# Attention backward of a branchformer layer: dP products in groups of four key chunks, with the remainder channels at four row positions of TensorE

## The chip, the cores and the metric

The kernel runs on one core of a Trainium2 chip. The metric is the device time of one launch in microseconds (us), the median of several runs. A profiled execution, taken by the hardware profiler, shows every instruction with its engine, line, start and duration. The engines are called PE (TensorE, matrix products; PEld are its weight loads), DVE (VectorE), ACT (ScalarE), POOL (GpSimd) and SP (SyncE, which here issues DMAs).

## The reference

The layer has two branches, attention and a gated convolution, which are merged by a depthwise convolution and a product. The kernel returns the output and the gradients of all eight inputs. Sizes: B = 2 sequences, T = 4000 tokens, D = 144 channels, K = 5 taps, all in bfloat16. What matters here is the attention and its gradient:

```python
xa = _layernorm(x, axis=-1)
qkv = jnp.einsum('btd,de->bte', xa, w_qkv)
q, k, v = (qkv[..., :D].copy(), qkv[..., D:2 * D].copy(), qkv[..., 2 * D:].copy())
scores = jnp.einsum('btd,bsd->bts', q, k) * D ** (-0.5)
p = _softmax(scores, axis=-1)
attn = jnp.einsum('bts,bsd->btd', p, v)
glob = jnp.einsum('btd,de->bte', attn, w_att_out)
...
return x + jnp.einsum('btc,cd->btd', m, w_merge)

def reference(x, w_qkv, ..., grad_out):
    _out, _vjp = jax.vjp(_f, x, w_qkv, w_att_out, w_mlp_in, dw_csgu, w_mlp_out, dw_merge, w_merge)
    _grads = _vjp(grad_out)
    return (_out, *_grads)
```

The backward pass needs, for every query block, the probabilities P (after the scores), dP = (gradient of attn) times v transposed, and dS = (dP - delta) * P, where delta is a number for each query.

## The kernel before, in words

Each sequence is cut into NB = 32 blocks of PB = 125 tokens (tokens are dealt out so that a block has one token of each partition's run). A query block is called a tile. The keys of a sequence are taken in eight chunks of CH = 500 columns, and two chunks make a pair. The key and value weights are folded into the query side, so that scores and dP are both products of a small transposed query tile with the normalized input `xa`, transposed. D = 144 does not fit the 128 rows of PE: the first 128 channels lie in `xaT_m` (128 x 4000), and the other DR = 16 in rows 0 to 15 of `R` (128 x 4000; its rows 16 to 111 hold the remainder channels of the output gradient for other products). Every product over the channels is therefore two matmuls: one with `xaT_m` and one with `R`, whose query side has zeros in the rows that don't count.

The two sequences are worked one after the other: a prologue (layernorm, transposes), then the attention loop `phase_att`, then a merge. Inside the loop, a few steps of one tile are:

- `jit_mm(i)` (L648) forms the query side `qb` (125 x 2 x 256; index 0 for scores, index 1 for dP; columns 144 to 255 are zero) in PSUM, and ACT copies it to one of three buffers. `jit_tr(i)` (L660) transposes it on PE into `qt` with four slots of 125 columns: slots 0 and 1 are main channels and remainder of the scores, slots 2 and 3 those of dP.
- `S_pair(i, c2)` (L673): four matmuls for a pair of chunks (L683 main, L684 remainder), a DVE operation of 1000 columns with a running minimum (L688, L690), and an exponential on ACT (L691) into `Pbuf`.
- `rescale(i)` (L693) brings earlier pairs to the final maximum (L700, L702) and starts a transposing DMA of P on SP's queue (L703).
- `Y_half(i, h)` (L705): 32 matmuls in two halves over the transposed P, then the reciprocal of the row sums, delta, and copies.
- `dP_pair(i, c2)` (L727): four matmuls for a pair of chunks, main and remainder alternating (L733, L734), then two DVE operations of 500 columns that form dS in `Sbuf` (L739).
- `Z_half` (L749), the same as Y over the transposed dS, and `zt_tr`.
- `X_group` (L780): products that gather the gradient of `xa` for three key blocks over the last two tiles (L794), added to `acc` by DVE (L800).
- `local(upto)` (L809) draws on a list of units of the convolution branch, so many as the share of the loop that has passed.

In iteration t the loop writes out the scores of tile t, Y and dP of tile t-1, Z of tile t-2 and X of tiles t-3 and t-2, in eight steps (L826 to L856): score pairs in steps 0 to 3, dP pairs in steps 4 to 7, and the other work between them. A planner turns this order into each engine's instruction order: it may draw an instruction ahead where an earlier one would have to wait, by its own estimates.

The PSUM pool `ps_sg` (L627) has two buffers of two banks each. A score pair and a dP pair each take one; a buffer comes free when the exponential (scores) or the dS operations (dP) have read it. The pool `ps_w` (three buffers) serves the other products, and `ps_yz` Y and Z.

In the prologue, `xat(g)` (L340) transposes `xa` and writes `xaT_m` and `R` for 1000 columns. SP's queue carries in the loop the transposing DMAs of P and dS and the stores of Y, Z and `ug`; in the prologue of the second sequence also the loads of `xo` and the stores of the first sequence's output.

Of the kernel before, what the change touches and what calls it, by code (L numbers as in the profile page):

```python
# [7 lines left out]
BF = mybir.dt.bfloat16  # L8
F32 = mybir.dt.float32
ACT = mybir.ActivationFunctionType  # L10
ALU = mybir.AluOpType
# [4 lines left out]
DR = 16  # L16
PB = 125
CH = 500
# [275 lines left out]
def pre_pieces(k, W, b, S, pst):  # L294
# [4 lines left out]
    if True:  # L299
# [49 lines left out]

        def go_rem():  # L350
            nc.gpsimd.tensor_copy(S.go_r[:], go_q[:, :, 128:D])
# [264 lines left out]
def phase_att(k, W, b, S, A, M):  # L616
# [6 lines left out]
    with ExitStack() as es:  # L623
# [20 lines left out]
        xaTm, R, xaa = S.xaT_m, S.R, S.xa_aug  # L644
# [3 lines left out]
        def jit_mm(i):  # L648
# [8 lines left out]
            nc.scalar.copy(qb[:, :, 0:D], pj[:].rearrange("p (a b) -> p a b", b=D))  # L657
            QB[i] = qb
# [68 lines left out]
        def dP_pair(i, c2):  # L727
            qt = QT[i]
            ps = ps_sg.tile([PB, 2, 512], F32, tag="sg")
            for h in range(2):  # L730
                c = 2 * c2 + h
                cs = slice(c * CH, (c + 1) * CH)
                nc.tensor.matmul(ps[:, h, 0:CH], qt[:, 2, :], xaTm[:, cs], start=True, stop=False)  # L733
                nc.tensor.matmul(ps[:, h, 0:CH], qt[:, 3, :], R[:, cs], start=False, stop=True)  # L734
            for h in range(2):
                c = 2 * c2 + h
                psrc = Pbuf[0:PB, i % NPB, c * 512:(c + 1) * 512].rearrange("p (a b) -> p a b", b=128)[:, :, 0:PB]
                sdst = Sbuf[0:PB, i % NDB, c * 512:(c + 1) * 512].rearrange("p (a b) -> p a b", b=128)[:, :, 0:PB]
                nc.vector.scalar_tensor_tensor(sdst, ps[:, h, 0:CH].rearrange("p (a b) -> p a b", b=PB), DL[i][:], psrc, op0=ALU.subtract, op1=ALU.mult)  # L739
# [63 lines left out]
        def ok(i):  # L803
            return 0 <= i < NB
# [11 lines left out]
        for t in range(NB + 1):  # L816
# [5 lines left out]
            def x(n):  # L822
                for _ in range(n):
                    if xg:
                        X_group(*xg.pop(0))
            for s in range(8):  # L826
                if s < 4 and ok(t):
                    S_pair(t, s)
                if s >= 4 and ok(t - 1):
                    dP_pair(t - 1, s - 4)  # L830
                if t == NB and s == 4:
                    M.late_y()
                if s == 0:
                    if ok(t - 3):
                        zt_tr(t - 3)
                    x(1)
                elif s == 1:
                    if ok(t + 1):
                        jit_mm(t + 1)
                    x(1)  # L840
                elif s in (2, 3):
                    if ok(t - 1):
                        Y_half(t - 1, s - 2)
                    if s == 3 and ok(t):
                        rescale(t)
                elif s == 4:
                    if ok(t + 1):
                        jit_tr(t + 1)
                    x(1)
                elif s == 5:  # L850
                    x(1)
                else:
                    if ok(t - 2) and t < NB:
                        Z_half(t - 2, s - 6)
                    x(1)
                local(-(-n_units * (8 * t + s + 1) // (8 * (NB - 1))))  # L856
# [415 lines left out]
def kernel(ctx, tc, x, w_qkv, w_att_out, w_mlp_in, dw_csgu, w_mlp_out, dw_merge, w_merge, grad_out,  # L1272
# [20 lines left out]
    R = bx.tile([128, T], BF, name="R")  # L1293
    go_r = bx.tile([PB, NB + 6, DR], BF, name="go_r")
# [7 lines left out]
    for b, S in enumerate(SS):  # L1302
        S.xaT_m, S.R, S.go_r, S.goT, S.acc, S.rstd_x = xaT_m, R, go_r, goT, acc, rstd[b]
        for nm in ("Yn", "ug", "Zn"):
            setattr(S, nm + "_d", tc.dram_tile([PB, NB, D], BF, name="%s_d%d" % (nm, b)))
# [155 lines left out]
```

## Time and profile before

| | |
|---|---|
| median of 3 runs | 1478.05 us (1475.49 to 1479.26) |
| profiled execution, device time | 1477.11 us |
| its span, first to last instruction | 1475.3 us |
| mean granted clock of PE | 0.985 |
| matmuls | 16184 |
| busy, share of the span | PE 93%, PEld 80%, DVE 82%, ACT 58%, POOL 19% |
| attention loop of the first sequence | about 59 to 660 us |
| attention loop of the second sequence | about 768 to 1370 us |

Busy times come from one execution. A matmul's recorded duration holds its latency in the array; what it costs PE is the distance from its start to the start of the next one. Lines such as L734 are those of the kernel file before the change. In a group of instructions, "x512" is the count, followed by the busy time in us and the mean duration of one in ns, and after the next bar the idle time of the engine just ahead of them with what ended it.

### The profile page before, as it was taken

The page shows a single profiled execution, that of the slowest core. Times are in us where ns is not written, and L with a number is a line of the kernel's source. Part 1 is how long each engine was busy: PE and PEld are TensorE (multiplying, and loading weights), DVE is VectorE, ACT ScalarE, POOL GpSimd, SP SyncE. Part 2 cuts the span into 40 slices and gives each one's busy share as a digit, 9 for nine tenths or more (in the row PEclk, how much of TensorE's full clock was granted, in tenths as well). Part 3 has the DMA queues.
Part 4 walks back from the last instruction along what each step waited for, and adds up shares of the span by engine and source line. Part 5 has one row for each costly group of instructions (what it writes and reads, how often), then busy time and mean ns, then how long its engine had stood idle before and what let it go on. Part 6 is the DMA issues. An engine that isn't in the chain of part 4 may idle for free. (4 is left out here: it accounts for less than half of the span.)

```text
span 1475.3 us, 39163 instructions
## 1 busy us (share of the span) xinstructions
PE 1377.6 (93%) x16184; PEld 1181.5 (80%) x16184; DVE 1217.1 (82%) x3060; ACT 849.7 (58%) x1538; POOL 282.0 (19%) x494
## 2 busy tenths in 40 slices
PE   2789999999999999997888999999999999999898
PEld 1568888888888888887885888888888888888797
DVE  6699888988898988887638998889898889888754
ACT  1666666666566656632637666666566656555182
POOL 8210111010111110026521112120101010101420
PEclk9899999999999999998999999999999999999999
DMA  3176667666666765578225776677667666677812
GB/s 101 31 144 121 121 121 122 120 122 117 118 115 113 119 118 111 107 138 209 62 56 104 138 122 113 111 121 124 119 123 121 121 121 121 116 117 124 218 35 64
DMA packets 559360, 170.44 MB, mean 116 GB/s; under 512 B 542443, under 2 KB 554093, under 8 KB 559136
## 3 DMA queue, kind: packets, MB, share of 16 engines
q1 hardware_dynamic: 553338, 155.43, 57.1%
q0 software_dynamic: 4768, 12.14, 3.2%
q8 instruction: 126, 2.06, 0.6%
q10 hardware_dynamic: 1076, 0.38, 0.1%
q14 instruction: 52, 0.43, 0.1%
HBM read 21.07 MB, written 14.16 MB: 24 GB/s over the span
## 5 line engine op out<-in xcount | busy, mean ns | idle before, releaser
L739 DVE SCALAR_TENSOR_TENSOR Sbuf<-ps,delta,Pbuf 125x500 bf16<-125x500 f32 x512 | 356.0, 731 | 28.2 <-PE ps L734 25.4
L794 PE MATMUL X<-QBs,Sbuf 125*125 125x144 bf16 x2048 | 303.1, 226 | 6.7 <-DVE acc L800 3.0
L794 PE MATMUL X<-QBs,Pbuf 125*125 125x144 bf16 x2048 | 302.1, 226 | 0.0
L794 PEld LDWEIGHTS <-Pbuf 125*125 125x125 bf16 x2048 | 262.1, 137 | 14.9 <-issue 10.3
L794 PEld LDWEIGHTS <-Sbuf 125*125 125x125 bf16 x2048 | 261.9, 137 | 7.7 <-DVE Sbuf L739 2.0
L800 DVE TENSOR_TENSOR acc<-X,acc 125x432 f32<-125x432 f32 x372 | 203.4, 550 | 33.0 <-PE X L794 31.9
L683 PE MATMUL ps<-xaT_m,qt 128*125 128x500 bf16 x512 | 194.6, 380 | 11.2 <-ACT Pbuf L691 9.9
L733 PE MATMUL ps<-xaT_m,qt 128*125 128x500 bf16 x512 | 192.7, 376 | 8.0 <-ACT Pbuf L691 5.7
L684 PE MATMUL ps<-R,qt 128*125 128x500 bf16 x512 | 194.0, 379 | 0.0
L734 PE MATMUL ps<-R,qt 128*125 128x500 bf16 x512 | 191.2, 373 | 0.0
L711 PEld LDWEIGHTS <-PT 125*125 125x125 bf16 x2048 | 147.9, 137 | 24.3 <-DMA PT<-Pbuf 6.5
L755 PEld LDWEIGHTS <-ST 125*125 125x125 bf16 x1984 | 144.2, 138 | 18.1 <-DMA ST<-Sbuf 0.6
L711 PE MATMUL yz<-xa_aug,PT 125*125 125x145 bf16 x2048 | 151.1, 227 | 4.1 <-DMA PT<-Pbuf 4.0
L755 PE MATMUL yz<-xa_aug,ST 125*125 125x144 bf16 x1984 | 147.8, 228 | 0.4 <-DMA ST<-Sbuf 0.4
L684 PEld LDWEIGHTS <-qt 128*125 128x125 bf16 x512 | 70.8, 138 | 33.3 <-issue 14.2
L734 PEld LDWEIGHTS <-qt 128*125 128x125 bf16 x512 | 69.8, 136 | 27.7 <-issue 8.2
L547 POOL TENSOR_TENSOR A_dwc<-l_fl,A_dwc 128x512 f32<-128x512 f32 (+2 forms) x48 | 35.7, 744 | 292.8 <-ACT l_fl L546 292.8
L688 DVE TENSOR_SCALAR_CACHE_REDUCE Pbuf<-ps 125x1000 bf16<-125x1000 f32 x64 | 76.6, 1197 | 14.5 <-PE ps L684 14.3
L733 PEld LDWEIGHTS <-qt 128*125 128x125 bf16 x512 | 70.0, 137 | 23.1 <-DVE Sbuf L739 2.7
L683 PEld LDWEIGHTS <-qt 128*125 128x125 bf16 x512 | 70.6, 138 | 21.9 <-issue 1.3
L759 ACT ACTIVATE zn<-yz,rl 125x144 bf16<-125x144 f32 x64 | 24.2, 378 | 108.5 <-PE yz L755 108.5
L417 POOL TENSOR_SCALAR l_a<-l_sq 125x576 bf16<-125x576 bf16 x32 | 21.4, 670 | 292.6 <-ACT l_sq L415 252.9
(807 smaller groups left out, 3055.1 us busy)
## 6 DMA issues: line engine op xcount, KB each, us to landing
Yn_d<-yn SPq DMA_DIRECT2D x64, 35.2 KB
Zn_d<-zn SPq DMA_DIRECT2D x64, 35.2 KB
ug_d<-ugr SPq DMA_DIRECT2D x32, 70.3 KB
xo<-in_x_dram SPq DMA_DIRECT2D x16, 140.6 KB
out_dram<-dxo SPq DMA_DIRECT2D x16, 140.6 KB
go_h<-in_grad_out_dram POOLq DMA_DIRECT2D x4, 504.0 KB, 6.8
Zn<-Zn_d SPq DMA_DIRECT2D x4, 504.0 KB
PT<-Pbuf SPq DMA_TRANSPOSE x64
```

Of the source, the lines that this page charges most:

```text
L547: nc.gpsimd.tensor_tensor(acc, fl[0:rows, 0:n], acc, op=ALU.add)
L683: nc.tensor.matmul(ps[:, h, 0:CH], qt[:, 0, :], xaTm[:, cs], start=True, stop=False)
L684: nc.tensor.matmul(ps[:, h, 0:CH], qt[:, 1, :], R[:, cs], start=False, stop=True)
L688: nc.vector.tensor_scalar(pdst, src, -1.0, None, op0=ALU.mult, op1=ALU.min, accum_out=nm[:, 0:1])
L711: nc.tensor.matmul(Y, PT[0:PB, j, 0:PB], xaa[:, j, 0:D + 1], start=(j == 0), stop=(j == NB - 1))
L733: nc.tensor.matmul(ps[:, h, 0:CH], qt[:, 2, :], xaTm[:, cs], start=True, stop=False)
L734: nc.tensor.matmul(ps[:, h, 0:CH], qt[:, 3, :], R[:, cs], start=False, stop=True)
L739: nc.vector.scalar_tensor_tensor(sdst, ps[:, h, 0:CH].rearrange("p (a b) -> p a b", b=PB), DL[i][:], psrc, op0=ALU.subtract, op1=ALU.mult)
L755: nc.tensor.matmul(Z, ST[0:PB, j, 0:PB], xaa[:, j, 0:D], start=(j == 0), stop=(j == NB - 1))
L759: nc.scalar.activation(zn[:, 0:D], Z, ACT.Copy, scale=RL.pop(i)[:])
L794: nc.tensor.matmul(X[:, jj, :], l, r, start=(n_ == 0), stop=(n_ == len(ops) - 1))
L800: nc.vector.tensor_tensor(av, X[:, 0:nj, :], av, op=ALU.add)
```

## The change

It changes the dP step and what it reads.

- In the prologue, each 500-column chunk of the remainder rows `R[0:16]` is also copied by a DMA of SP's queue into a new tile `XR` (128 x 2 x 500): chunk c goes to rows 32*(c % 4) and those after, plane c // 4.
- In `jit_mm`, a POOL copy repeats the 16 remainder channels of the dP side three more times, at distances of 32 columns, so that after the transposes slot 3 of `qt` holds them at rows 0, 32, 64 and 96.
- `dP_pair` becomes `dP_quad`: it takes both `ps_sg` buffers, issues the four main matmuls of four chunks, then the four remainder matmuls, each with 16 rows at its own row position (0, 32, 64, 96) and into its own bank, and then two dS operations of 1000 columns in place of four of 500. The remainder matmuls are issued behind the last main one, with priority.
- The loop's eight steps are written out anew: there are two groups where four pairs were, Z_half follows each of them, and the X groups and the shares of the local units lie at other places. Score pairs are as they were.

```diff
             nc.vector.tensor_copy(v8(S.R, 8 * g, 8)[0:DR], pr[0:DR, :, 0:PB])
+
+            for c in (2 * g, 2 * g + 1):
+                r = 32 * (c % 4)
+                nc.sync.dma_start(S.XR[r:r + DR, c // 4, :], S.R[0:DR, c * CH:(c + 1) * CH])
...
             nc.scalar.copy(qb[:, :, 0:D], pj[:].rearrange("p (a b) -> p a b", b=D))
+            rem_ = qb[:, 1, 128:256].rearrange("p (r c) -> p r c", c=32)[:, :, 0:DR]
+            nc.gpsimd.tensor_copy(rem_[:, 1:4, :], rem_[:, 0:1, :].to_broadcast([PB, 3, DR]))
             QB[i] = qb
...
-        def dP_pair(i, c2):
+        def dP_quad(i, m):
+
             qt = QT[i]
-            ps = ps_sg.tile([PB, 2, 512], F32, tag="sg")
-            for h in range(2):
-                c = 2 * c2 + h
-                cs = slice(c * CH, (c + 1) * CH)
-                nc.tensor.matmul(ps[:, h, 0:CH], qt[:, 2, :], xaTm[:, cs], start=True, stop=False)
-                nc.tensor.matmul(ps[:, h, 0:CH], qt[:, 3, :], R[:, cs], start=False, stop=True)
-            for h in range(2):
-                c = 2 * c2 + h
-                psrc = Pbuf[0:PB, i % NPB, c * 512:(c + 1) * 512].rearrange("p (a b) -> p a b", b=128)[:, :, 0:PB]
-                sdst = Sbuf[0:PB, i % NDB, c * 512:(c + 1) * 512].rearrange("p (a b) -> p a b", b=128)[:, :, 0:PB]
-                nc.vector.scalar_tensor_tensor(sdst, ps[:, h, 0:CH].rearrange("p (a b) -> p a b", b=PB), DL[i][:], psrc, op0=ALU.subtract, op1=ALU.mult)
+            pp = [ps_sg.tile([PB, 2, 512], F32, tag="sg", name="ps") for _ in range(2)]
+            for r in range(4):
+                c = 4 * m + r
+                mm = nc.tensor.matmul(pp[r // 2][:, r % 2, 0:CH], qt[:, 2, :], xaTm[:, c * CH:(c + 1) * CH], start=True, stop=False)
+            with tc.issue_after(mm.ins), tc.high_priority():
+                for r in range(4):
+                    rs = slice(32 * r, 32 * r + DR)
+                    nc.tensor.matmul(pp[r // 2][:, r % 2, 0:CH], qt[rs, 3, :], XR[rs, m, :], start=False, stop=True)
+            for c2, ps in enumerate(pp, 2 * m):
+                psrc = pchunk(i % NPB, c2).rearrange("p (h a b) -> p h a b", h=2, b=128)[:, :, :, 0:PB]
+                sdst = Sbuf[0:PB, i % NDB, c2 * 1024:(c2 + 1) * 1024].rearrange("p (h a b) -> p h a b", h=2, b=128)[:, :, :, 0:PB]
+                nc.vector.scalar_tensor_tensor(sdst, ps[:, :, 0:CH].rearrange("p h (a b) -> p h a b", b=PB), DL[i][:], psrc, op0=ALU.subtract, op1=ALU.mult)
...
+            def loc(f):
+                local(-(-int(n_units * (t + f) * 1000) // (1000 * (NB - 1))))
+            if ok(t):
+                S_pair(t, 0)
+            if ok(t - 3):
+                zt_tr(t - 3)
+            x(1)
+            loc(0.2)
+            if ok(t):
+                S_pair(t, 1)
+            if ok(t + 1):
+                jit_mm(t + 1)
+            x(1)
+            loc(0.25)
+            if ok(t):
+                S_pair(t, 2)
+            if ok(t - 1):
+                Y_half(t - 1, 0)
+            loc(0.4)
+            if ok(t):
+                S_pair(t, 3)
+            if ok(t - 1):
+                Y_half(t - 1, 1)
+            if ok(t):
+                rescale(t)
+            loc(0.6)
+            x(1)
+            if ok(t - 1):
+                dP_quad(t - 1, 0)
+            if t == NB:
+                M.late_y()
+            if ok(t + 1):
+                jit_tr(t + 1)
+            if ok(t - 2) and t < NB:
+                Z_half(t - 2, 0)
+            loc(0.85)
+            x(1)
+            if ok(t - 1):
+                dP_quad(t - 1, 1)
+            if ok(t - 2) and t < NB:
+                Z_half(t - 2, 1)
+            loc(1.0)
             x(6)
...
+    XR = bx.tile([128, 2, CH], BF, name="XR")
```

More of the change, by code (lines that the diff above doesn't have):

```diff
@@ L643, in phase_att @@
             nc.gpsimd.memset(t_[:, D:256], 0.0)
-        xaTm, R, xaa = S.xaT_m, S.R, S.xa_aug
+        xaTm, R, XR, xaa = S.xaT_m, S.R, S.XR, S.xa_aug
         QT, QB, RL, DL, YZ, ZN, ZT, NM, DHT = {}, {}, {}, {}, {}, {}, {}, {}, {}
@@ L825, in x @@
                         X_group(*xg.pop(0))
[L826 to L856, printed above, removed]
+            def loc(f):
[40 more added lines that the diff above has]
+            loc(1.0)
             x(6)
@@ L1302 @@
     for b, S in enumerate(SS):
-        S.xaT_m, S.R, S.go_r, S.goT, S.acc, S.rstd_x = xaT_m, R, go_r, goT, acc, rstd[b]
+        S.xaT_m, S.R, S.XR, S.go_r, S.goT, S.acc, S.rstd_x = xaT_m, R, XR, go_r, goT, acc, rstd[b]
         for nm in ("Yn", "ug", "Zn"):
```

## The prediction, made before the changed kernel was run

> **What bounds the kernel now.** I read four views in this order: the page's engine sums, its slices, its groups by cost, and then the instructions of TensorE (PE) in order of time.
>
> The sums and the slices come first (busy us, share of the span, instructions; then tenths per slice).
>
> ```profile
> PE 1377.6 (93%) x16184; PEld 1181.5 (80%) x16184; DVE 1217.1 (82%) x3060; ACT 849.7 (58%) x1538; POOL 282.0 (19%) x494
> ...
> PE   2789999999999999997888999999999999999898
> ...
> PEclk9899999999999999998999999999999999999999
> ```
>
> PE is full nearly everywhere and its clock is granted. A busy PE could still be a PE that waits inside, so I asked for the two attention loops by themselves, and for what PE waits on there (us in all, times, longest).
>
> ```profile
> 140.00:620.00 480.00, 471.60 (x5501) 404.20 (x5500) 423.25 (x981) 299.32 (x539) 56.65 (x88) 1.00 0.66 119
> 850.00:1310.00 460.00, 451.77 (x5256) 386.77 (x5255) 407.67 (x944) 287.79 (x518) 61.27 (x100) 1.00 0.68 120
> ```
>
> ```profile
> PE ps L733 <- ACT Pbuf L691: 1.8, 4, 0.8
> PE X L794 <- DVE acc L800: 1.5, 2, 0.8
> PE ps L733 <- DVE Sbuf L739: 0.9, 3, 0.4
> ```
>
> The columns of the first two lines are PE, PEld, DVE, ACT, POOL, clock, DMA share and GB/s. Of 480 us PE is busy 472 and DVE 423 (88%); all waits of PE on others in that window come to 9 us. So a loop tile is paid in PE time, with DVE second at a distance of 12%. Start to start, the matmuls of a 125x144 product are 62 or 63 ns apart and those of 500 columns 210 (median over all of them): summed at that pace PE has 462 of 480 us to stream. A tile takes 18.67 us (mean over 60 tiles).
>
> Then the groups that the change touches (busy us, mean ns of one, idle before).
>
> ```profile
> L739 DVE SCALAR_TENSOR_TENSOR Sbuf<-ps,delta,Pbuf 125x500 bf16<-125x500 f32 x512 | 356.0, 731 | 28.2 <-PE ps L734 25.4
> L733 PE MATMUL ps<-xaT_m,qt 128*125 128x500 bf16 x512 | 192.7, 376 | 8.0 <-ACT Pbuf L691 5.7
> L734 PE MATMUL ps<-R,qt 128*125 128x500 bf16 x512 | 191.2, 373 | 0.0
> ```
>
> L734 multiplies only 16 channels that count, yet streams as long as L733. Its 373 ns hold latency; its cost is the 210 to the next start, 107.5 us over 512.
>
> The last view shows the one place where this trace has matmuls of 16 rows among full ones: small transposes near the end (start us, us, engine, line).
>
> ```profile
> 1406.29 0.22 PE L1129 MATMUL fpt<-ident,goT 128*128 128x128 bf16 x1
> 1406.45 0.18 PE L1130 MATMUL fpt<-ident,goT 16*128 16x16 bf16 x1
> 1406.56 0.23 PE L1129 MATMUL fpt<-ident,goT 128*128 128x128 bf16 x1
> 1406.72 0.18 PE L1130 MATMUL fpt<-ident,goT 16*128 16x16 bf16 x1
> 1406.83 0.49 PE L973 MATMUL Hps<-Yg,go_h 125*128 125x144 bf16 x5
> ```
>
> A 128-column matmul is followed after 58 ns by its like (L499) but after 154 by a 16-row one: entering costs 96 ns. The 16-row one streams 16 columns (7 ns) and its successor starts 109 after it: leaving costs 102. Weight loads, otherwise hidden, come after the gap.
>
> **The change part by part: PE.** Today the remainders of four chunks cost 4 x 210 = 840 ns. Afterwards a group pays 96 to enter, 208 for one stream of 500 columns, 102 to leave, and two bare weight loads: the 16-row transpose with an 80-column load (L1136) lasts 198 ns against 178, and the 80-column product behind it 257 against 226, so 20 to 31 ns each, about 30 for 125 columns; 60 together. That is 466. The other three matmuls have no row here. If all four stream at once they add nothing; if their loads follow one another they add at most 3 x 62 = 186, the distance at which 125-column loads start in X (L794); if their streams follow one another they add 3 x 210 = 630. I take the middle of the first two, 559, because loads have a row that paces them and nothing in the 16-row rows shows a whole stream being waited for, beyond what entering and leaving cost. The saving is 840 - 559 = 281 ns a group, two groups for each of 64 tiles: 128 x 0.281 = 36.0 us. Its ends are 374 (47.9 us) and 188 (24.1 us); the third bound, a loss of 256 ns a group, is a rival below. All of it lies on the path, since PE has no slack to lose it in. The four main products are the same four, at the same 210 to 213.
>
> A sentence beside this: the Trainium skill ("TensorE: Matmul & The Clock Gate", Part 3, Packing small matmuls) gives a measured speedup of 3.07 for four row tiles of 512 columns. By it the four would take 840 / 3.07 = 274 ns, with the 198 of switching and 30 of the last load 502, an estimate that would save 338 a group and make the sum below 1448. No run here shows it yet.
>
> **DVE.** Eight operations of 500 columns start 646 ns apart when queued. The accumulating add (L800) takes 600 ns at 432 columns and 298 at 144, 1.05 ns a column, so 500 more columns cost 525 and one of 1000 about 1171. Per tile 8 x 646 - 4 x 1171 = 0.48 us less, 31 us in all; the 1000-column reduce (L690), 1182 start to start, gives 0.44. The other end is no gain, if the operation pays for each of its two pieces. It is off the path while DVE is 88% busy, so I count nothing; it pays for the longer bursts below.
>
> **Hand-over of the score buffers.** This is where a stall can go. There are two PSUM buffers of two chunks, and a group takes both. Its third main matmul waits for the buffer of the last score pair, or, in the second group, for the second dS operation of the first; queued behind it on PE are the four remainders, jit_tr and everything later. First group: the exponential that frees the buffer ends 2.87 us (median; mean 3.07, upper quarter from 3.26) after the start of the last score matmul. PE has until then 0.21 of that matmul, 1.01 for Y, 0.51 for a fifth of the tile's 2.55 us of local units, 0.75 for an X group, 0.42 for two mains: 2.90. Mean wait, with 0.05 for the signal: 0.22. Second group: the first dS operation starts 0.75, 1.33, 1.48 and 0.85 us after the last dP matmul of the four pairs, mean 1.10; the second ends 1.17 + 1.26 later, 3.58 with the signal. PE has 0.34 to finish and leave, 0.22 jit_tr, 1.01 Z, 0.64 local, 0.75 X, 0.42 mains: 3.38. Mean wait 0.20. Together 0.42 a tile, against 0.21 that PE loses ahead of L733 today (5.2 us over 25 tiles of start-to-start excess). Ends: 0 more, if the order is filled as it is now (in a quarter of the tiles the third dP pair follows the second at once, the X group having been drawn ahead), and 0.42 more. I take the difference, 0.21 x 64 = 13.4 us lost.
>
> **Small pieces.** The copy on POOL repeats 48 columns: nearest row, the 64-column copy (L459), 0.24 us, 64 times, on an engine idle 88% of the loop. What hides it: qb is written at 443.8 and transposed at 448.5, over 4 us. Queued behind the power at L436, whose input comes from the layernorm, it could make jit_tr wait up to 0.7 us in every other tile, 22 us; I take 0. The eight small DMAs of a batch go into SP's queue behind each group's copy of R; in the first batch that queue is empty from 44 to 70 us, in the second the loads of xo and stores of o stand behind them, at 0.3 to 0.4 us an issue: 3 us if exposed, I take 0. Z_half moves ahead by about one dP pair and an X group, some 2 us; the transposing DMA that it needs is issued at 438.85 with 4.83 us and Z starts at 452.89, so 9 us of cover remain 7. The X groups and the shares of local units only move.
>
> **Sum.** The profiled execution took 1477.11 us, span 1475.3 and 1.8 around it. 1477.1 - 36.0 + 13.4 = 1454.5; the median of the runs lies 0.9 higher, so 1455. Its own range: 1430 (47.9 saved, no wait more) to 1480 (24.1 saved, 0.42 more).
>
> **Rivals.**
> *The four positions do not overlap* (slower; also the case that the change doesn't do what it says). Then a group takes 466 + 630 = 1096 instead of 840, and 128 x 0.256 = 32.8 us come on top: 1511. It decides from two of the four streams serial: 466 + 210 still saves 164, 466 + 420 loses 46. For it: no matmuls at different row positions overlap anywhere in this trace, and the switch shows that rows are a mode with a price. Against: the 16-row transposes show that the gap belongs to the change between row sizes, and four positions of one size have none between them.
>
> *Both buffers in one hand* (slower). If DVE or ACT reach the groups as late as they do today in the upper quarter, first group 3.31 - 2.90 = 0.41, second 1.78 + 2.48 - 3.38 = 0.88, then 1.29 - 0.21 = 1.08 us a tile are lost, 69 us against 36 gained: 1511. It decides at 0.56 us a tile. For it: dP starts with only 50 ns of slack after its buffer comes free in a tenth of the tiles or more, and bursts of 2.4 us on DVE hold up the adds of X behind them. Against: median slack is 0.5 to 1.2 us, and DVE has 0.48 us a tile less to do. The Trainium skill ("TensorEngine Tiling (Array Packing)", PSUM Bottleneck) warns that tiling speeds the products and not the emptying of PSUM; the waits ahead of L739 (25 us on PE, not the reverse) do not show that bound yet.
>
> *Gain and waits cancel* (no change): the slow end of saving with the whole 0.42: 1477 to 1481.
>
> **How the numbers follow.** A measurement of this kernel can tell about 0.3%, 4.4 us, from no change. Forecast 0.64, cancelling 0.08, no overlap 0.13, both buffers 0.15. Faster 0.64, same 0.08, slower 0.28. The range from 1430 to 1506 holds the forecast, no change, and about half of the buffer rival; it leaves out serial positions and a still better overlap.
>
> **What would show it.** Right: the four remainder matmuls start within some 60 ns of one another; from the last main's start to the next full-row matmul 0.7 to 0.9 us, against 1.05 for one main and four remainders today; 256 dS operations near 1250 ns; PE's busy sum down by tens of us with L733's count unchanged; the tile period near 18.3 us. Wrong: remainders 210 ns apart (first rival), or idle time ahead of the third main of a group, put down to the exponential or to dS, above 0.5 us a tile (second).

## The result, and the profile after

The forecast was 1455 us, faster. The changed kernel takes 1484.29 us (median of 9 runs, 1481.99 to 1490.65), the kernel before 1479.15 (9 runs, 1475.49 to 1482.76): a ratio of 1.0041, with a 95% interval of 1.0027 to 1.0056. It is slower by about 5 us. Its profiled execution took 1483.08 us, with a span of 1480.8 against 1475.3.

In the kernel file after the change the score matmuls are L689 and L690, their exponential L697, the rescale on DVE L706, the dP mains L739, the remainders L743, and dS L747.

The page of the kernel after, engine sums and slices:

```profile
PE 1347.8 (91%) x16184; PEld 1125.0 (76%) x16184; DVE 1189.3 (80%) x2804; ACT 850.0 (57%) x1538; POOL 300.2 (20%) x558
...
PE   2789999999999999988887999999999999999798
...
PEclk9999999999999999999998999999999999999999
```

PE has 30 us less to do and DVE 28, as meant, in a span that is 5.5 longer. So the time went into waiting. The two attention loops by themselves, kernel after (PE, PEld, DVE, ACT, POOL, clock, DMA share, GB/s):

```profile
140.00:620.00 480.00, 460.82 (x5511) 382.58 (x5509) 414.37 (x887) 299.62 (x540) 63.75 (x114) 1.00 0.65 119
850.00:1310.00 460.00, 441.15 (x5269) 365.68 (x5267) 399.43 (x856) 285.79 (x517) 67.87 (x124) 1.00 0.67 121
```

PE's idle time in the first window was 8.4 us of 480 and is now 19.2. What it waits for there (us, times, longest), kernel after:

```profile
PE ps L739 <- ACT Pbuf L697: 7.2, 12, 1.5
PE ps L739 <- DVE Sbuf L747: 4.2, 9, 0.8
PE X L802 <- DVE acc L808: 3.2, 7, 0.7
```

The dP mains stood behind these two releasers for 2.7 us before; it is 11.4 now. The groups that were changed, kernel after:

```profile
L747 DVE SCALAR_TENSOR_TENSOR Sbuf<-ps,delta,Pbuf 125x1000 bf16<-125x1000 f32 x256 | 311.0, 1253 | 16.1 <-PE ps L743 16.1
...
L739 PE MATMUL ps<-xaT_m,qt 128*125 128x500 bf16 x512 | 144.5, 377 | 38.9 <-ACT Pbuf L697 20.2 <-DVE Sbuf L747 16.7
...
L706 DVE TENSOR_SCALAR Pbuf<-Pbuf,f 125x1000 bf16<-125x1000 bf16 x128 | 56.5, 485 | 33.8 <-ACT f L702 33.5
L743 PE MATMUL ps<-XR,qt 16*125 16x500 bf16 x512 | 55.2, 421 | 0.0
```

The rescale on DVE in the kernel before:

```profile
L700 DVE TENSOR_SCALAR Pbuf<-Pbuf,f 125x1000 bf16<-125x1000 bf16 x128 | 55.8, 479 | 9.3 <-ACT f L696 8.5
```

The idle time ahead of the mains went from 8.0 to 38.9 us, and nearly all of it (20.2 and 16.7) ends with the two releasers that hand over the score buffers. DVE itself now waits 33.5 us for the factor `f` of the rescale, which ACT makes (8.5 us before). One tile in order of time shows how this hangs together. PE of the kernel after (start us, us, then the idle time before and its releaser):

```profile
450.99 0.59 PE L739 MATMUL ps<-xaT_m,qt 128*125 128x500 bf16 x2
452.36 0.58 PE L739 MATMUL ps<-xaT_m,qt 128*125 128x500 bf16 x2 [0.79 <-ACT Pbuf L697]
452.88 0.43 PE L743 MATMUL ps<-XR,qt 16*125 16x500 bf16 x4
453.24 0.39 PE L671 MATMUL pt<-ident,qb 125*128 125x125 bf16 x4
```

ACT of the same kernel:

```profile
451.21 1.10 ACT L697 ACTIVATE Pbuf<-ps,nm__6905 125x1000 bf16<-125x1000 f32 x1 [0.64 <-DVE Pbuf L696]
...
452.89 0.29 ACT L702 ACTIVATE f<-nm__6905 125x3 f32<-125x3 f32 x1
```

DVE of the same kernel:

```profile
453.22 0.88 DVE L706 TENSOR_SCALAR Pbuf<-Pbuf,f 125x1000 bf16<-125x1000 bf16 x2 [0.80 <-ACT f L702]
454.01 2.42 DVE L747 SCALAR_TENSOR_TENSOR Sbuf<-ps,delta,Pbuf 125x1000 bf16<-125x1000 f32 x2
```

The third main waits 0.79 for the exponential that frees its buffer, which ends at 452.31. All four remainders are under way at once, and PE goes on 0.36 us after they start. The group's dP is ready when the remainders end at 453.31, and dS starts at 454.01: DVE has first to wait for `f` and to do the two rescales. The time that the four positions saved on PE is over before DVE comes.

**An account by tiles.** For each sequence I take the stretch from the first score matmul of tile 3 to that of tile 29 (steady, 52 tiles in both), the ramp from tile 0 to tile 3, and the rest. Every matmul counts at the pace of its columns (211 ns for 500, 62.5 for 144), and what lies beyond that before the next start counts as a wait ahead of the next one. The account is of one execution of each kernel.

| us | before | after |
|---|---|---|
| per steady tile: streaming, without the 16-row matmuls | 18.11 | 16.45 |
| 16-row matmuls and what is lost in front of them | | 0.72 + 0.19 |
| waits ahead of dP mains | 0.20 | 0.72 |
| waits ahead of score mains | 0.06 | 0.18 |
| other waits | 0.37 | 0.45 |
| small differences | 0.15 | 0.13 |
| tile, mean | 18.89 | 18.84 |
| 52 steady tiles | 982.4 | 979.5 |
| both ramps | 84.8 | 92.8 |
| from tile 29 to the next sequence's tile 0 | 177.7 | 178.4 |
| start to first tile, and from tile 61 on | 59.4 + 171.0 | 57.5 + 172.6 |

So 0.75 us a tile were saved on PE and 0.72 given back in waits, and on top of that the two ramps grew by 8.0.

The ramp can be seen in the first iterations. Kernel before, PE, the second iteration's Y and first dP matmul, then the first score matmul of the next tile:

```profile
75.93 0.37 PE L733 MATMUL ps<-xaT_m,qt 128*125 128x500 bf16 x1 [0.82 <-ACT Pbuf L691]
...
77.83 2.24 PE L711 MATMUL yz<-xa_aug,PT 125*125 125x145 bf16 x32 [1.10 <-DMA PT<-Pbuf]
...
84.96 0.37 PE L683 MATMUL ps<-xaT_m,qt 128*125 128x500 bf16 x1
```

The same places after:

```profile
75.60 0.58 PE L739 MATMUL ps<-xaT_m,qt 128*125 128x500 bf16 x2 [0.82 <-ACT Pbuf L697]
78.14 3.88 PE L717 MATMUL yz<-xa_aug,PT 125*125 125x145 bf16 x32 [1.95 <-DMA PT<-Pbuf]
...
84.15 0.58 PE L739 MATMUL ps<-xaT_m,qt 128*125 128x500 bf16 x2 [1.35 <-DVE Sbuf L747]
...
88.84 0.34 PE L717 MATMUL yz<-xa_aug,PT 125*125 125x145 bf16 x2 [1.69 <-DMA PT<-Pbuf]
89.02 0.38 PE L689 MATMUL ps<-xaT_m,qt 128*125 128x500 bf16 x1
```

Here there is no Z yet and hardly any X that could fill gaps. Before, three dP matmuls ran ahead of Y and five behind it; after, only two mains can start, since the rest of the group needs the buffer of the last scores, and Y waits 0.85 us longer for its transposing DMA (1.95 against 1.10). The second group then waits 1.35 for dS, and the next scores stand behind a Y that waits 1.69 for its transposing DMA. Besides, the 32 products of Y take 3.88 instead of 2.24 us. The granted clock says why (after the length of the stretch stand PE, PEld, DVE, ACT, POOL and the clock), kernel before and then after:

```profile
76.00:80.00 4.00, 2.90 (x36) 2.38 (x36) 1.97 (x6) 3.90 (x6) 0.04 (x1) 1.00 0.41 96
80.00:84.00 4.00, 3.46 (x31) 2.41 (x29) 3.89 (x12) 1.20 (x3) 1.25 (x3) 1.00 0.75 141
```

```profile
76.00:80.00 4.00, 2.05 (x18) 1.87 (x18) 3.52 (x15) 3.43 (x6) 1.35 (x3) 0.80 0.19 37
80.00:84.00 4.00, 2.80 (x23) 2.26 (x23) 1.71 (x4) 0.85 (x2) 0.15 (x1) 0.77 0.21 41
```

### The profile page after: what moved, and what is told of

It is laid out like the page before. It is cut to its first block, busy times and chain, and to the rows that moved or that the text cites. A ratio compares the mean times of both kernels' runs of the same rounds, so it can differ in the third digit from the quotient of the medians.

```text
span 1480.8 us, 38973 instructions
## 1 busy us (share of the span) xinstructions
PE 1347.8 (91%) x16184; PEld 1125.0 (76%) x16184; DVE 1189.3 (80%) x2804; ACT 850.0 (57%) x1538; POOL 300.2 (20%) x558
## 4 chain that ended last, share of the span: by engine, by line
PE 39%; DVE 31%; ACT 13%; issue 6%; DMA 6%; POOL 5%; DVEq 0%; POOLq 0%; SPq 0%; ACTq 0%
DVE Sbuf L747 10%; PE X L802 7%; DVE Pbuf L696 7%; ACT Pbuf L697 4%; PE ps L689 4%; PE ps L690 4%; PE yz L717 3%; PE yz L763 3%; DVE acc L808 3%; PE po L1071 3%; DMA PT<-Pbuf 3%; PE ps L739 2%; DVE Pbuf L694 2%; PE Hps L992 1%; DVE Pbuf L706 1%
## 5 line engine op out<-in xcount | busy, mean ns | idle before, releaser
L747 DVE SCALAR_TENSOR_TENSOR Sbuf<-ps,delta,Pbuf 125x1000 bf16<-125x1000 f32 x256 | 311.0, 1253 | 16.1 <-PE ps L743 16.1
L802 PE MATMUL X<-QBs,Sbuf 125*125 125x144 bf16 x2048 | 298.4, 227 | 9.0 <-DVE acc L808 7.3
L802 PE MATMUL X<-QBs,Pbuf 125*125 125x144 bf16 x2048 | 297.3, 226 | 0.0
L802 PEld LDWEIGHTS <-Pbuf 125*125 125x125 bf16 x2048 | 262.1, 137 | 15.5 <-issue 14.0
L689 PE MATMUL ps<-xaT_m,qt 128*125 128x500 bf16 x512 | 195.8, 382 | 14.1 <-ACT Pbuf L697 12.2
L690 PE MATMUL ps<-R,qt 128*125 128x500 bf16 x512 | 195.2, 381 | 0.0
L739 PE MATMUL ps<-xaT_m,qt 128*125 128x500 bf16 x512 | 144.5, 377 | 38.9 <-ACT Pbuf L697 20.2
L763 PEld LDWEIGHTS <-ST 125*125 125x125 bf16 x1984 | 135.9, 138 | 16.6 <-issue 14.7
L739 PEld LDWEIGHTS <-qt 128*125 128x125 bf16 x512 | 62.3, 137 | 65.3 <-issue 53.7
L690 PEld LDWEIGHTS <-qt 128*125 128x125 bf16 x512 | 71.0, 139 | 39.0 <-issue 19.6
L689 PEld LDWEIGHTS <-qt 128*125 128x125 bf16 x512 | 70.9, 139 | 21.2 <-issue 2.1
L706 DVE TENSOR_SCALAR Pbuf<-Pbuf,f 125x1000 bf16<-125x1000 bf16 x128 | 56.5, 485 | 33.8 <-ACT f L702 33.5
L708 ACT ACTIVATE Pbuf<-Pbuf,f 125x1000 bf16<-125x1000 bf16 x64 | 72.8, 1137 | 0.6
L777 ACT COPY zt<-pt 128x250 bf16<-128x250 bf16 x64 | 23.3, 365 | 73.9 <-PE pt L775 73.3
```

What stands on the lines that cost most here:

```text
L689: nc.tensor.matmul(ps[:, h, 0:CH], qt[:, 0, :], xaTm[:, cs], start=True, stop=False)
L690: nc.tensor.matmul(ps[:, h, 0:CH], qt[:, 1, :], R[:, cs], start=False, stop=True)
L706: nc.vector.tensor_scalar(pdst, pdst, f[:, c2:c2 + 1], None, op0=ALU.mult)
L708: nc.scalar.activation(pdst, pdst, ACT.Copy, scale=f[:, c2:c2 + 1])
L739: mm = nc.tensor.matmul(pp[r // 2][:, r % 2, 0:CH], qt[:, 2, :], xaTm[:, c * CH:(c + 1) * CH], start=True, stop=False)
L747: nc.vector.scalar_tensor_tensor(sdst, ps[:, :, 0:CH].rearrange("p h (a b) -> p h a b", b=PB), DL[i][:], psrc, op0=ALU.subtract, op1=ALU.mult)
```

## The experiments

Each kernel ran beside the kernel before, whose median was 1479.0, 1479.8, 1479.1 and 1478.9 in the four batches; the ratios and their intervals are against these. "Steady" and "ramps" are those of the account and come from one execution, whose time stands in the column "profiled". Single executions of one kernel lie up to 12 us apart (e14), so small steps in these two columns count only where several kernels show them.

| kernel | median us | ratio (95%) | profiled | steady, 52 tiles | ramps |
|---|---|---|---|---|---|
| before | 1479.15 | | 1477.11 | 982.4 | 84.8 |
| after | 1484.29 | 1.0041 (1.0027 to 1.0056) | 1483.08 | 979.5 | 92.8 |
| e1_full_rows | 1491.28 | 1.0079 (1.0061 to 1.0097) | 1491.86 | 991.6 | 90.9 |
| e2_pairs_new_order | 1485.43 | 1.0053 (1.0035 to 1.0070) | 1481.95 | 982.9 | 92.8 |
| e3_dS_before_rescale | 1492.47 | 1.0093 (1.0078 to 1.0108) | 1492.25 | 976.4 | 96.8 |
| e4_x_ahead | 1477.40 | 0.9993 (0.9984 to 1.0003) | 1476.85 | 974.1 | 92.3 |
| e5_before_rescale_act | 1503.08 | 1.0167 (1.0134 to 1.0200) | 1510.04 | 992.4 | 95.6 |
| e6_after_rescale_act | 1505.77 | 1.0186 (1.0161 to 1.0211) | 1505.38 | 990.9 | 96.9 |
| e7_full_rows_rescale_act | 1521.07 | 1.0277 (1.0251 to 1.0304) | 1522.33 | 1003.5 | 96.4 |
| e8_x_ahead_rescale_act | 1496.39 | 1.0115 (1.0095 to 1.0135) | 1495.11 | 982.8 | 97.2 |
| e9_all_x_ahead | 1485.58 | 1.0040 (1.0024 to 1.0055) | 1478.62 | 965.6 | 93.7 |
| e10_local_ahead | 1473.86 | 0.9960 (0.9943 to 0.9978) | 1474.83 | 969.6 | 93.4 |
| e11_after_no_dve_rescale | 1468.77 | 0.9925 (0.9896 to 0.9954) | 1467.19 | 965.9 | 89.9 |
| e12_full_rows_no_dve_rescale | 1485.30 | 1.0039 (1.0022 to 1.0056) | 1486.31 | 985.2 | 92.0 |
| e13_before_no_dve_rescale | 1469.45 | 0.9937 (0.9916 to 0.9959) | 1470.06 | 975.1 | 84.5 |
| e14_old_start | 1475.23 | 0.9975 (0.9962 to 0.9987) | 1483.49 | 978.9 | 86.1 |
| e15_old_start_local_ahead | 1468.64 | 0.9932 (0.9910 to 0.9955) | 1471.79 | 970.0 | 84.8 |
| e16_old_start_all_x_ahead | 1478.09 | 0.9994 (0.9981 to 1.0007) | 1478.24 | 966.4 | 85.4 |

**First batch: the parts of the change, and two ways to give the buffers more time.** e1 keeps groups and order, but multiplies the remainders over full rows as before (without the copy on POOL):

```diff
-                    nc.tensor.matmul(pp[r // 2][:, r % 2, 0:CH], qt[rs, 3, :], XR[rs, m, :], start=False, stop=True)
+                    nc.tensor.matmul(pp[r // 2][:, r % 2, 0:CH], qt[:, 3, :], R[:, c * CH:(c + 1) * CH], start=False, stop=True)
```

> The changed kernel, its groups of four chunks, its order and its dS of 1000 columns kept, but each remainder matmul reads all 128 rows of R as before, one behind the other, and the POOL copy is gone (the small DMAs stay). Three theories. Ring: a tile of the changed kernel is closed by the round trip of the two score buffers (last exponential, third main, remainders, dS, third main of the second group, next scores), and the PE time that the row positions save became waits of PE. Remainders lie on this ring: 840 ns a group in place of the 455 that the trace shows, 128 x 0.385 = 49 us slower than the changed kernel, about 1533 us. PE time: the row positions save nothing in truth, the trace's starts 4 ns apart only hide it, and full rows cost the same: within 8 us of 1484. Order: the new order of the loop costs what the positions save; like the ring, about 1530.

Measured: 1491.28, only 7.0 us above the changed kernel, where a saving that shows in full would have put it near 1530. By the number alone this fits the theory that the positions save nothing (within 8 us of 1484); but the trace of e1 has its remainders 210 ns apart where the changed kernel has 4, so PE's time is saved. The waits ahead of dP mains fall from 0.72 to 0.51 us a tile, those ahead of scores from 0.18 to 0.10 and the others from 0.45 to 0.18: 0.56 of the 0.75 us that the positions save are taken from waiting. One distance shows it best. From the third main of the first group to the start of its dS it is 1.65 us in both kernels: 0.52 to the start of the last remainder and 1.13 from there with four positions, 1.06 and 0.59 with full rows (means of the steady tiles). There DVE starts when it is ready, not when PE is. (e1 also lacks the POOL copy, for which PE waits 2.8 us in the whole of the changed kernel.)

e2 keeps the new order, with the old pairs in it:

```diff
         def dP_quad(i, m):
+            dP_pair(i, 2 * m)
+            dP_pair(i, 2 * m + 1)
```

> The changed kernel's order of the loop, but each group is made of two dP pairs as before: four matmuls of full rows and two dS operations of 500 columns each, each pair with one buffer; no POOL copy. Ring: the first pair needs only one buffer and hands it on before the second is done, so PE streams as before the change and waits little: 1470 to 1490 us. Order: if the order of the loop is what costs, this shows it alone: about 1525 us (45 us over the kernel before). PE time: 1479, the kernel before.

Measured: 1485.43. Its steady tiles are as long as before (982.9 against 982.4), and its ramps are those of the changed kernel to the tenth. So the new order alone costs 8 us in the ramps and leaves the steady tiles as they were. Its median is 6.3 us above the kernel before and 1.1 from the changed kernel: the net loss is that of the order, and groups and positions together bring nothing that can be told from no change. From e2 to e1, which makes groups of the pairs, with dS in operations of 1000 columns, the steady tiles grow by 8.7; from e1 to the changed kernel, which adds the row positions and their copy on POOL, they shrink by 12.1. No run separates the groups from the longer dS operations.

e3 issues the rescale on DVE behind the first dS of the first group:

```diff
-            if ok(t):
-                rescale(t)
             loc(0.6)
             x(1)
             if ok(t - 1):
-                dP_quad(t - 1, 0)
+                ds = dP_quad(t - 1, 0)
+            if ok(t):
+                with tc.issue_after(ds.ins):
+                    rescale(t)
```

> The changed kernel with DVE's two rescale operations of a tile held until the first group's two dS operations are issued (they stand ahead of them now). Ring: the first dS starts 1.13 us after the last remainder where 0.41 is possible; up to 0.7 us a tile of the ring goes, 64 x 0.4 to 0.7 = 25 to 45 us faster than the changed kernel, 1440 to 1460 us, and PE's idle time ahead of the third main of the second group falls. PE time: DVE has the same work, nothing changes: 1480 to 1488. Order: 1480 to 1488.

Measured: 1492.47, a miss. dS does start earlier (0.60 us behind the last remainder in place of 1.13), but from the first group to the second it shortens only from 4.32 to 4.18 us, the steady stretch by 3.1, while the ramps, the passage between the sequences and the end lose 4.0, 3.3 and 4.9. The transposing DMA of P is issued later, and PE's waits for it ahead of Y grow from 7.4 to 14.2 us in the whole run; 5.8 of the 14.2 lie at the ends of the two sequences (2.1 at 655 us, 3.7 at 1376). In the ramps these waits hardly grow; what makes them longer was not settled.

e4 draws one more X group ahead of the first group:

```diff
             loc(0.6)
-            x(1)
+            x(2)
```

> The changed kernel with one X group (0.75 us of PE) moved from the end of the iteration, between the second group and the next scores, to ahead of the first group, where PE waits for the last exponential. PE does the same work. Ring: the stretch from the second group to the next scores (3.5 us, with 0.9 us of slack on its buffer) gets shorter by 0.75 and the wait ahead of the third main takes it up in part: 0.3 to 0.7 us a tile, 1440 to 1465 us. PE time: the same work in another order, 1480 to 1488. Order: a change either way.

Measured: 1477.40, no different from the kernel before, and 6.9 below the changed one. The steady tiles give 5.4 of that. The expected 1440 to 1465 was not reached.

**Second batch: DVE relieved by ACT.** Pairs 0 and 1 are rescaled on ACT, as pair 2 is; e5 is that in the kernel before, e6 in the changed one, e7 in e1, e8 in e4:

```diff
-                if c2 < 2:
-                    nc.vector.tensor_scalar(pdst, pdst, f[:, c2:c2 + 1], None, op0=ALU.mult)
-                else:
-                    nc.scalar.activation(pdst, pdst, ACT.Copy, scale=f[:, c2:c2 + 1])
+                nc.scalar.activation(pdst, pdst, ACT.Copy, scale=f[:, c2:c2 + 1])
```

> The kernel before the change, with the two rescale operations that DVE does for each tile (0.43 us each, start to start) done by ACT like the third. After the first four runs the ring theory has to be told anew: with full rows the time from the third main to the first dS is the same 1.65 us as with row positions (1.06 + 0.59 against 0.52 + 1.13), so dS starts when DVE comes to it, not when the remainders end. DVE queue theory: PE bounds the old kernel and DVE's instruction queue the changed one. Then here, where PE bounds, 0.86 us a tile less for DVE gives little: 1470 to 1480 us. If DVE's load already bounded the kernel before: 1425 to 1450. PE theory (PE bounds both): 1479.

> The changed kernel with the rescale on ACT alone. DVE queue theory: the rescale stands ahead of the first dS on DVE in the changed kernel and waits there for its factor; without it dS starts about 0.6 us after the last remainder in place of 1.13, DVE has 0.86 us a tile less, and 0.4 to 0.8 us a tile go: 1435 to 1460 us. PE theory: 1480 to 1488. Ring of buffers alone, without regard to DVE: 0.53 a tile, 1450.

> As the last but with the remainders over full rows, one after the other. It tells what the row positions are worth once DVE is relieved. DVE queue theory: with DVE out of the way PE's 0.77 us a tile (0.385 a group) begin to show: 20 to 45 us slower than the changed kernel with rescale on ACT. If the remainders still don't matter: within 10 us of it, as before the relief (1491 against 1484).

> The changed kernel with both edits: one X group ahead of the first group and the rescale on ACT. DVE queue theory: the two gains add in part (X ahead gave 7 us alone): 1425 to 1455 us, faster than both kernels. PE theory: 1477.

Measured: 1503.08, 1505.77, 1521.07 and 1496.39; all slower than without the edit, by 19 to 30 us. e5, e6 and e8 miss every range that was named for them, and e7 falls between its two. In e6 dS starts 0.57 us behind the remainders and the groups follow each other 3.81 us apart, as hoped, but a rescale takes 1128 ns on ACT against 485 on DVE, ACT is busy for 96% of the time between the first and the last dP main of a tile (76% in the changed kernel), and the work that it owes seems to come back later; where, was not traced. The edit does not help; still, two things follow. The rescale in front of dS does hold up the groups (4.32 us apart with it, 3.81 without). And with DVE relieved, the row positions are worth 15.3 us (e7 to e6) instead of 7.0.

**Third batch: more work ahead of the groups, and the rescale left out.** e9 is e4 with a second X group ahead of the second group as well. e10 is e4 with all the local units that are due drawn ahead of the second group:

```diff
-            x(1)
+            x(2)
             if ok(t - 1):
                 dP_quad(t - 1, 0)
 ...
-            loc(0.85)
+            loc(1.0)
             x(1)
             if ok(t - 1):
                 dP_quad(t - 1, 1)
```

> The changed kernel with one X group moved ahead of the first group (as in the run with X ahead, 1477 us) and the last X group moved from behind the second group to ahead of it. Hand-over theory, as it stands now: the row positions do save 0.75 us of PE a tile (that sum is read from the trace), and the waits ahead of the third mains and of the next scores take it back because what PE has to do between two hand-overs no longer covers the round through DVE and ACT. With X ahead, PE idles 0.88 us a tile between the two groups, and the buffers have 0.8 us of slack between the second group and the next scores; moving 1 us of work over evens them: 0.3 to 0.6 us a tile, 1440 to 1462 us. Conserved-idle theory (PE and DVE, each in its own order, cost each other about 1.6 us a tile wherever the work stands): 1474 to 1482.

> As with X ahead, and the last share of the local units (15 in 100, about 0.4 us of PE a tile, and their DVE work with them) drawn ahead of the second group. Hand-over theory: 0.1 to 0.3 us a tile less than with X ahead alone, 1458 to 1471. Conserved idle: 1474 to 1482.

Measured: e9 has by far the shortest steady stretch, 965.6, with the waits ahead of dP mains down to 0.20 us a tile; but those ahead of scores rise to 0.63, and all waits together, with 0.20 elsewhere, fall only from 1.35 to 1.03: most of the wait moved from the mains to the scores. Its profiled execution, which loses 8.0 between the sequences, took 1478.62, the shortest of its ten; what makes the median 7 us longer, at 1485.58, is not seen. e10 comes to 1473.86, the first that beats the kernel before, at the edge of what was named for a wait that only moves (1474 to 1482). What PE waits for in its first loop, kernel e10:

```profile
PE ps L739 <- DVE Sbuf L747: 6.9, 14, 0.8
PE ps L739 <- ACT Pbuf L697: 2.4, 5, 0.8
```

The wait for the exponential is down from 7.2 to 2.4 us, since PE has more to do before the first group's third main; what is left is dS, the hand-over to the second group, whose waits rise from 4.2 to 6.9.

e11 leaves out the two DVE multiplications that bring pairs 0 and 1 to the final maximum, in the changed kernel; e12 does so in e1, and e13 in the kernel before:

```diff
-                if c2 < 2:
-                    nc.vector.tensor_scalar(pdst, pdst, f[:, c2:c2 + 1], None, op0=ALU.mult)
-                else:
+                if c2 == 2:
```

> The changed kernel without DVE's two rescale operations (pairs 0 and 1 of P are left unscaled; ACT's third is kept): DVE has 0.86 us a tile less, ACT nothing more, unlike the runs with the rescale on ACT, where ACT had no idle time left in the dP stretch. DVE queue theory (dS starts when DVE comes to it): 0.5 to 0.8 us a tile, 1430 to 1455 us. If DVE is not what the groups wait for: 1478 to 1486.

> The same left out, with the remainders over full rows, one after the other. If PE's saving is hidden only because DVE is late, it shows here: 25 to 45 us slower than the changed kernel with the same left out. If something else hides it: within 12 us of that kernel.

> The kernel before the change without DVE's two rescale operations (pairs 0 and 1 of P left unscaled): the control for the same cut in the changed kernel, which took 15 us off it. PE bounds the old kernel: 1470 to 1480 us, at most half of that gain. If the old kernel is held by DVE as much as the new one: 1460 to 1466.

Measured: 1468.77 for e11, 15.5 below the changed kernel; 1485.30 for e12, so that the row positions are now worth 16.5 us; 1469.45 for e13, 9.4 below the kernel before. All three lie between the ranges named for their two theories. Without the 0.88 us a tile in which DVE rescales, the changed loop gains more than the old one, and PE's saving is better seen. But the old loop gains too, and e11 still keeps a wait of 0.54 us a tile ahead of the dP mains. So DVE's queue is a part of the cause and not the whole: scores, exponential, groups and dS wait for each other around two buffers, and taking time from one engine of that round shortens it only by a part. No run gives the pool a third buffer, so that two buffers are too few is argued and not shown.

**Fourth batch: the ramps.** e14 is the changed kernel with the old order and the old pairs in the first two iterations of a sequence; e15 adds the edits of e10, e16 those of e9:

```diff
+            if t < 2:
+                for s in range(8):
+                    if s < 4 and ok(t):
+                        S_pair(t, s)
+                    if s >= 4 and ok(t - 1):
+                        dP_pair(t - 1, s - 4)
 ...
+            else:
```

> The changed kernel, but in iterations 0 and 1 of each sequence the loop has the old order, and dP of the first tile is done in pairs with full rows (without the copies on POOL for that tile). The traces put 4 to 5 us of the loss in each sequence between the scores of tile 1 and those of tile 2. Start theory: these come back, 5 to 9 us, 1475 to 1480 us. If the start only shifts a loss that comes later: 1482 to 1486.

> The old order in iterations 0 and 1 with one X group and the last share of local units ahead of their groups (that alone: 1474). If the two repairs add: 1464 to 1470 us, faster than the kernel before by more than 0.5%. If they overlap: 1472 to 1476.

> The old order in iterations 0 and 1 with both X groups ahead (that alone 1486, though its steady tiles are the shortest of all, 18.57 us; it lost 10 us between the two sequences). If that loss lies in the first two iterations: 1460 to 1470 us. If it lies elsewhere: 1478 to 1486.

Measured: e14 1475.23, 9.1 below the changed kernel; the ramps are back at 86.1, with the steady stretch unchanged (the profiled execution of e14 took 1483.49, the longest of its ten; against the changed kernel it is longer by 3.9 us between the sequences, 2.3 at the start and 1.9 at the end, not in what is read here). So the changed tiles with the old start beat the kernel before by 3.7 us. The Y of the first ramp is under the halved clock in e14 too, though it waits less than in the kernel before:

```profile
78.67 3.88 PE L718 MATMUL yz<-xa_aug,PT 125*125 125x145 bf16 x32 [1.03 <-DMA PT<-Pbuf]
```

So that halved stretch is not what e14 removes.

e15 1468.64: both repairs add up, and it is the best of all, 10.2 us below the kernel before. Its steady stretch is 970.0 and its ramps 84.8. e16 is at 1478.09, in the range named for a loss that does not lie in the first iterations: steady tiles and ramps are short, but from tile 29 to the next sequence's tile 0 it takes 191.5 us against 177.9 in e15, with waits of 6.2 and 3.1 us for two steps of the merge and the granted clock at 0.89 from 690 to 770 us against 0.98 from 690 to 760 in e15. Why X groups that are drawn ahead do this was not settled.

## Why the prediction was wrong

**The four positions** went right, and at the good end. The remainders start 4 ns apart, 10 ns from first to last. From the last main to the first remainder it is 304 ns, 93 more than a main takes (forecast 96 to enter), and 351 from the last remainder to the next matmul. A group costs 454 ns, the 466 of the sum with nothing for the other three, where I took 559. Streams and loads of the other three hide fully; the 93 ns that I had put on their loads were not there. That saves 0.386 us a group by these distances (49 us) and 0.75 us a tile by the account (48 us), the upper end of that term. The first rival (no overlap, 1511) is out. The Trainium skill ("TensorE: Matmul & The Clock Gate", Part 3, Packing small matmuls) gives starts about 4 ns apart, and this trace agrees; by its 3.07 a group would have cost an estimated 502 with the switching, and the measured 454 lies under that.

**DVE** went right: 1000-column operations start 1169 ns apart (forecast 1171), and DVE's load in the first window fell from 423 to 414 us.

**The hand-over of the score buffers** is the step that failed, and with it the sentence that all of PE's saving lies on the path. The sum lost 0.42 us a tile there, less 0.21 lost before: 0.21 net. Measured in the account: 0.52 net ahead of the dP mains, 0.12 ahead of scores and 0.08 elsewhere, 0.72.

The times in its working were near. In the steady tiles of the changed kernel the exponential that frees a buffer ends 3.10 us after the start of the last score matmul (forecast 3.07), and PE has 2.84 us of work until the third main (2.90). The second dS operation ends 3.56 us after the start of the last remainder (3.53), and PE has 3.53 us of work until the second group's third main (3.38). What was wrong is the step from these times to a wait: it took one mean from another. With the measured means and 0.05 for the signal that gives 0.31 and 0.08, together 0.39; measured are waits of 0.40 and 0.27, together 0.67. In a tile where the buffer comes late PE waits, and where it comes early nothing is given back: the end of the exponential has a median of 2.81 and an upper quarter from 3.41. The 0.20 ahead of scores and elsewhere had no term.

The round also explains why a larger saving on PE brought a longer wait. It makes PE arrive earlier at the next hand-over, where ACT and DVE are no earlier: the 1.65 us from the third main to dS are the same with and without the row positions (e1). The forecast of 1.10 us from the last matmul to dS came out (1.13), but it was taken over without asking why: the rescale stands in front of dS on DVE, waiting for a factor from ACT. The saving was added up on PE as if PE alone paced the tile, because it was 98% busy. e1, e7 to e6 and e12 to e11 show that it did not: 7.0, 15.3 and 16.5 us of 48 reach the end, each uncertain by some 3 to 5 us.

**The rivals.** The one that came closest is that gain and waits cancel, which I gave 0.08 with 1477 to 1481; it stood for a small saving with the whole wait, whereas here a large saving met a larger wait. The rival with both buffers in one hand had the right place, and waits there did take back the saving. But its condition, DVE and ACT as late as in the upper quarter, did not come true (their means are as forecast). It put 1.08 us a tile on the mains and said it decides from 0.56; 0.52 was measured there and 0.72 with the other waits, against a saving of 0.75 and not 0.56, so that the steady tiles still come out 3 us shorter. That 1484 lies in the range from 1430 to 1506 is due to the half of this rival that the range took in; the sum's own range ended at 1480.

**The ramps** had no term at all. The sum moved the X groups, Z and the local units as free, which holds in the steady tiles (e2: 982.9 against 982.4); in the first iterations of each sequence, where there is little to fill gaps with, the order costs 8.0 us. That alone turned a loop that had gained 3 us into a kernel that lost 5; with the old start (e14) the changed kernel is 3.7 us faster than the one before.

**The small pieces** are as taken. PE is said to have waited 2.8 us on the POOL copy in the whole run; the 16 new DMAs of the prologue last 576 ns each in the median, and the time from the start to the first tile is 57.5 us against 59.4; Z waits for nothing (0.0 us idle ahead of it).

**What would show it.** Remainders within 60 ns: 10. From the last main to the next full-row matmul 0.7 to 0.9 us: 0.67, a little better still. The dS operations near 1250 ns: 1253. PE's sum down by tens of us: 29.8. These signs came; the tile near 18.3 us did not. That figure goes with the 18.67 of the prediction, a mean over 60 tiles; the steady tiles of the account took 18.89 before, from which the same 0.35 less (0.56 saved, 0.21 lost) makes 18.54, and 18.84 was measured. The idle time ahead of the third mains, the sign named for the second rival, is 0.67 us a tile and so over its 0.5.

## What to carry to other kernels

When a loop hands two buffers round between three engines, a saving on the busiest one is not yet a saving of the loop: add up the round (filling, reading, release), ask on which engine's queue the next release stands and behind what, count the spread from tile to tile and not only the means, and expect a part. A step that takes all buffers at once needs other work placed ahead of it that lasts until the buffers come free; drawing such work forward (e10) was worth 10 us here. And a new order is to be priced in the first and last iterations by itself, where nothing fills its gaps; keeping the old order there (e14) cost nothing and gave 9 us back.

## What the runs showed of the hardware that was not expected

Four 16-row matmuls of 500 columns at four row positions start within 10 ns and cost 454 ns a group, with 93 ns to get in and about 140 to get out (351 less the 211 of a stream), against 840 for four over full rows. Neither the streams nor the weight loads of the other three show.

In the ramp of the first sequence the granted clock fell to a half for stretches of 3.4 us (71.6 to 75.0 and 78.4 to 81.8 in the kernel after, only 72.4 to 75.8 before), each behind a stretch of that length in which PE had been idle for much but not all of the time: 2.2 and 2.5 us of 3.4 in the kernel after, 2.0 before. The Trainium skill ("TensorE: Matmul & The Clock Gate", Part 1: The HAM clock gate) has windows of about 3.4 us and a halved clock after an idle one; the length agrees, but a window need not be wholly idle. Under the halved clock Y's 32 products took 1.64 us more. That the longer wait of Y brought this about is not shown: in e14 Y waits 1.03 us, less than the 1.10 in the kernel before, and the halved stretch (78.8 to 82.2) falls on its products all the same.
